# Moving the sums of accumulators by two steps, and reordering the first steps, in a state-space scan joined to a gated MLP

## The chip, the cores and the metric

The kernel runs on one core of a Trainium2 chip. The metric is the device time of one execution in microseconds (us). A core has engines with instruction queues of their own: TensorE (PE in the profile, its weight loads PEld), VectorE (DVE), ScalarE (ACT), GpSimd (POOL) and SyncE (SP, which here only issues DMAs). They wait for one another by semaphores.

## The reference

Two blocks follow each other. The first is a chunked state-space scan over 4 sequences, 8 heads, 768 positions, head width 32 and state width 16. With `C`, `B`, `x` and a decay `a` per position, each chunk gives

```python
M = (C @ B.T) * L                      # L: causal products of decays
y = M @ x + (C @ state) * decay_to_i
state = decay_full * state + sum((B x) * decay_from_j)
```

Its output, arranged as 3072 tokens of width 256, goes into the second block:

```python
h = x @ w_in          # 256 -> 2048
g = h * np.cos(h)
out = g @ w_out       # 2048 -> 256
```

All is float32.

## The kernel before

The 768 positions are cut into six chunks of 128 (the first of them again into two half chunks). Each chunk has 512 tokens over the four sequences. The second block of chunk c is done in 16 steps f = 0 to 15; step n = 16c + f works on 256 of the 512 tokens and on 256 of the 2048 hidden columns. Each step has, in this order of dependence:

- `first(n)` (L705): TensorE multiplies by a part of `w_in` into a PSUM bank `hp`. From step 4 on the `hp` of a step takes one of two banks in turn, so `first(n+2)` needs the bank of step n back.
- `wind_k` (L712, ScalarE) rounds h/2π to an integer `k`, `wind_w` (L718, VectorE) takes the fractional turn `w`, `gate` (L727, ScalarE) takes the cosine as a shifted sine, and `gated` (L732, VectorE) writes `gT` = h cos h from `hp`, after which the bank is free.
- `second(n)`, issued two steps later (`LAG` = 2): TensorE multiplies `gT` by a part of `w_out` into accumulators. In chunk 0 it is a plain product (L776). In chunks 1 to 5 it is a seven-product scheme (`seven`, L814), which needs differences `gd` of `gT`, made by POOL (L757 to L760).

At the last step of each half (f = 7 and f = 15, `second` of which is issued at the end of steps f = 9 and f = 1 of the next chunk), ScalarE copies the seven accumulators to SBUF (L823, L824, tile `ps`) and a closure is put on a list `unsummed`: four VectorE adds (L831, tile `sum`) and two output DMAs (L834). The list is emptied by every step after its `gated`.

While the steps of chunk c - 1 run, the scan of chunk c is woven in. The four sequences go in two pairs, at f = 7 and f = 11. At the end of the step before (f = 6, f = 10): two `reach` scans (L552) and two 32x32 block transposes (L575) on VectorE. In the step: two scaled copies `cT` on ScalarE (L585), `rT` on VectorE (L587), and after the step's `second` 32 small matmuls `g` on TensorE (L602, `intra2`). The masks `m` (L623, VectorE) of a pair's two sequences follow at the end of the next step and in the step after that, ahead of its `gated`. At the end of f = 14 `finish2` multiplies them: `y` (L637, L644), sums for the state (L665).

The two weights are fetched by SP in eight pieces each (in 0 to 7, out 0 to 7) and rounded in the first steps: `grade` takes an absolute value (ScalarE, L254), a clip (POOL, L255) and, as `rest`, a scaled remainder (ScalarE, L252); `join` takes a shift (VectorE, L267), a merge (VectorE, L269) and an addition (POOL, L277) that writes the piece of `w_in` or `w_out`. `first_steps` writes out by hand the order of steps 0 to 3, and the loop from step 4 (`AHEAD` = 4) continues. In step n the loop grades the piece of step n + 1 (odd steps have in (n+3)/2, even ones out n/2) and joins that of step n. `clip_all` (POOL, L920) clips the decays into `la`, which SP stores to DRAM (L923) for later loads. SP issues its DMAs strictly in the order in which the program emits them, and each engine its instructions likewise: no planner moves anything.

The state after the half chunk 1 is completed by `add_s` (POOL, L534 twice and L536), in before at step 6 (`AHEAD + 2`). It is read by `finish0` of half chunk 2 at the end of step 14.

Of the kernel before, what the change touches and what calls it, by code (L numbers as in the profile page):

```python
# [25 lines left out]
def kernel(  # L26
# [21 lines left out]
    NF = DF // P  # L48
# [169 lines left out]
    def kept(which, i):  # L218
        return (w_in[:, :, i * WC:(i + 1) * WC] if which == "in" else
                w_out[:, i * WF:(i + 1) * WF])  # L220
# [12 lines left out]
    held = {}  # L233

    def shares(which, ap, n):

        return [ap] if n == 1 else [ap.rearrange("p (k e f) -> p e k f", k=KT, e=n)[:, e]
                                    for e in range(n)]

    def grade(which, i, later=False, n=1):  # L240


        t = words.pop((which, i), None)
        if t is None:
            return
        mag = conv.tile([P, 2 * WC], FP32, tag="mag", bufs=3, name="mag")
        last = conv.tile([P, 2 * WC], U32, tag="last", bufs=3, name="last")
        low, high, mags, lasts = (shares(which, ap, n) for ap in (t[:, :, 0], t[:, :, 1], mag, last))
        held[which, i] = list(zip(high, shares(which, mag.bitcast(U32), n), lasts))

        def rest(e=0):
            ACT.activation(lasts[e], low[e], AF.Copy, scale=2.0 ** -29)  # L252
        for e in range(n):
            ACT.activation(mags[e], high[e].bitcast(FP32), AF.Abs)  # L254
            G.tensor_scalar(out=mags[e], in0=mags[e], scalar1=MOST, scalar2=LEAST,  # L255
                            op0=ALU.min, op1=ALU.max)
            if not later:
                rest(e)
        if later:
            return rest  # L260

    def join(which, i):


        parts = held.pop((which, i), ())
        for e, (high, bits, last) in enumerate(parts):
            V.tensor_scalar(out=bits, in0=bits, scalar1=3, scalar2=0x3FFFFFFF,  # L267
                            op0=ALU.logical_shift_left, op1=ALU.bitwise_and)
            V.scalar_tensor_tensor(out=bits, in0=high, scalar=0xC0000000, in1=bits,  # L269
                                   op0=ALU.bitwise_and, op1=ALU.bitwise_or)  # L270
            dst = kept(which, i)
            if len(parts) > 1:
                dst = dst[:, :, e * P:(e + 1) * P]
            else:
                bits, last = (ap.rearrange("p (k f) -> p k f", k=dst.shape[1])
                              for ap in (bits, last))
            G.tensor_tensor(out=dst.bitcast(U32), in0=bits, in1=last, op=ALU.add)  # L277
# [10 lines left out]
    for s in range(2):  # L288
# [3 lines left out]
        out=a_in, in_=a.rearrange("(u b) h (c p) -> (b h c) u p", u=NU, p=P))  # L292
# [417 lines left out]
    def wind_k(n):  # L710
        k = ffn.tile([P, TB], I32, tag="k", name="k")
        ACT.activation(k, hp[n], AF.Copy, bias=0.25, scale=INV_2PI)  # L712
        turns[n] = k
# [11 lines left out]
    def gate(n):  # L725
        cos = turns[n]
        ACT.activation(cos, cos, AF.Sin, bias=quarter, scale=TWO_PI)  # L727

    def gated(n):
        cos = turns.pop(n)  # L730
        gT[n] = ffn.tile([P, TB], FP32, tag="gT", bufs=LAG + 1, name="gT")
        V.tensor_tensor(out=gT[n], in0=hp.pop(n), in1=cos, op=ALU.mult)  # L732
        gT[n] = gT[n].rearrange("p (q m) -> p q m", q=4)
        if NF <= n < NC * NF - 1:
            differ(n)
# [104 lines left out]
    unsummed = []  # L840
# [78 lines left out]
    def clip_all():  # L919
        G.tensor_scalar(out=la, in0=a_in, **clip)  # L920
# [6 lines left out]
    piece = {n: ("in", (n + 3) // 2) if n % 2 else ("out", n // 2) for n in range(NF)}  # L927
# [16 lines left out]
    def units_at(n, i):  # L944
        return [k for k, at in unit_at.items() if at[i] == n]
# [47 lines left out]
    AHEAD = 4  # L993

    def first_steps():

        grade("in", 1)
        weigh0(1)
        for q in range(2):
            weights(1, q)  # L1000
        states_of = []
        first(0, lambda: states_of.extend(finish0(1)))
        take_s1, add_s1 = states_of
        join("in", 1)
        rests = [grade("out", 0, later=True)]
        wind_k(0)
        take_s1()
        rests.pop()()
        wind_w(0)
        first(1)  # L1010
        join("out", 0)
        wind_k(1)
        gate(0)
        wind_w(1)
        gate(1)
        gated(0)
        gated(1)
        first(2, tag=None)
        rests = [grade("in", 2, later=True)]
        wind_k(2)  # L1020
        rests.pop()()
        clip_cut()
        wind_w(2)
        rests = [grade("out", 1, later=True)]
        join("in", 2)
        first(3, tag=None)
        gate(2)
        wind_k(3)
        rests.pop()()
        join("out", 1)  # L1030
        gated(2)
        second(0)
        wind_w(3)
        clip_all()
        rests = [grade("in", 3, later=True)]
        gate(3)
        rests.pop()()
        gated(3)
        second(1)
        join("in", 3)  # L1040
        return add_s1

    add_s = first_steps()
    for k in (2, 3):
        G.memset(alongs[k][:, :, 0:1], 0.0)
    rest_of_loads()
    for n in range(AHEAD, NC * NF + LAG):
        c, f = divmod(n, NF)
        if n < NC * NF:

            if c > 0 and f == (NJ if c == 1 else 0):
                if c == 1:
                    load(2, only=(x,))
                load(c + 2)
            if n in (NF - 4, NF + 1):
                for b in range(2):
                    load_a(2, (2 * (n > NF) + b,))
                    load_along(2, (2 * (n > NF) + b,))
            first(n)
            wind(n)  # L1060
            for at in pairs(n):
                turn2(*at)
            for k in units_at(n, 2):
                turn_unit(k)
            rests = [grade(*piece[m], later=True)
                     for m in ((n,) if n == AHEAD else (n + 1,)) if m in piece]
            gate(n)
            for rest in rests:
                if rest:
                    rest()  # L1070
            joins = n > AHEAD and n in piece and piece[n] in held
            if joins:
                join(*piece[n])
            elif n == AHEAD:
                grade(*piece[n + 1])

            behind = [lambda at=at: halved(*at) for at in halves_at(n)]
            behind += [lambda k=k, p=p: decays0(k, p) for k, at in unit_at.items()
                       for p in range(2) if at[0][p] == n]
            behind = [lambda at=(c, 2 * u + 1): masked(*at) for c, u in pairs(n - 2)] + behind  # L1080
            behind = [lambda k=k: weights(k, 1) for k in units_at(n - 1, 3)] + behind
            if not joins and behind:
                behind.pop(0)()
            gated(n)
            if n == AHEAD:
                join(*piece[n])
            if add_s and (n == AHEAD + 2 or units_at(n - 1, 4)):
                add_s()
                add_s = None
            for do in (*behind, *unsummed):  # L1090
                do()
            unsummed.clear()
            for k, ((_, last_), *_) in unit_at.items():
                if last_ == n:
                    weigh0(k)
                    if k == 3:
                        units_of_decay()
        for i, js in differ_at.get(n, ()):
            differ_w(i, js)
        if n >= LAG:  # L1100
            second(n - LAG)
        for c, u in pairs(n - 1):
            intra2(c, u)
            masked(c, 2 * u)
        for k in units_at(n, 3):
            for t in range(2):
                inner(k, t)
            weights(k, 0)
        for k in units_at(n, 4):
            take_s, add_s = finish0(k)  # L1110
            take_s()
        for k in units_at(n, 1):
            reach_unit(k)
        for c, us in ends(n):
            finish2(c, us)
            if 1 in us:
                raw.pop(c)
        for c, u in pairs(n + 1):
            for b in (2 * u, 2 * u + 1):
                reaches(c, b)  # L1120
                load_along(c + 1, (b,))
            turn_blocks(c, u)
        for at, (c, u) in block_loads.items():
            if at == n:
                loading = load_blocks(c, u)
            if at <= n < at + 8:
                next(loading)
# [30 lines left out]
```

## Time and profile before

| What | us |
|---|---|
| median of 3 runs | 375.1 (374.86 to 375.34) |
| the profiled execution | 374.5 |
| its span, first to last instruction | 372.7 |
| TensorE busy in the span | 363.2 |
| VectorE busy | 274.3 |
| POOL busy | 215.6 |
| ScalarE busy | 172.6 |

The time of the profiled execution is of one run; its span leaves out what lies before the first and after the last instruction. Lines of the timeline give the start, the duration, the engine, the line of the kernel, the operation with the tile written and the tiles read, the number of instructions merged, and in brackets the idle time of the engine before it with what ended it. Ends of matmuls are modelled in the profile, so that periods between steps are read from starts.

### The profile page before, as it was taken

What the parts mean: (1) busy time and instruction counts of PE and PEld (TensorE: products, weight loads), DVE (VectorE), ACT (ScalarE), POOL (GpSimd) and SP (SyncE); (2) the same over time, 40 slices, a digit from 0 to 9 for tenths busy, and PEclk for the clock granted to TensorE, in tenths of its full rate; (3) what the DMA queues carried; (4) which work ended last, traced back from release to release, by engine and by line L of the source; (5) the groups of instructions that cost most, each with busy time, mean ns of one, the idle gap of its engine ahead of it and who ended that gap; (6) DMA issues with size and microseconds to landing.
All of it is one profiled execution on the core that took longest, in us unless ns stands there. A gap on an engine that the chain in (4) does not pass through costs nothing.

```text
span 372.7 us, 8684 instructions
## 1 busy us (share of the span) xinstructions
PE 363.2 (97%) x3390; PEld 326.6 (88%) x3390; DVE 274.3 (74%) x451; ACT 172.6 (46%) x299; POOL 215.6 (58%) x339
## 2 busy tenths in 40 slices
PE   8999999999999899999999999999999999999996
PEld 5787878889999799999899999899999989999995
DVE  7788998578699848977857987766987872544543
ACT  3678566553443434444335345433534443444442
POOL 6556855579776547765445684453685344544451
PEclk9999999999999999999999999999999999999999
DMA  9947796666077552530344340110010100010011
GB/s 145 296 163 185 163 272 88 117 162 167 5 144 132 139 76 66 151 91 0 70 55 93 91 135 16 49 24 2 11 38 2 25 5 2 2 28 1 2 30 29
DMA packets 96489, 30.49 MB, mean 82 GB/s; under 512 B 70240, under 2 KB 92352, under 8 KB 96448
## 3 DMA queue, kind: packets, MB, share of 16 engines
q1 hardware_dynamic: 94160, 29.48, 35.0%
q10 hardware_dynamic: 2288, 0.46, 0.6%
q8 instruction: 27, 0.44, 0.5%
q14 instruction: 14, 0.11, 0.1%
HBM read 26.58 MB, written 3.34 MB: 80 GB/s over the span
## 4 chain that ended last, share of the span: by engine, by line
PE 74%; DVE 10%; DMA 4%; ACT 4%; SPq 3%; issue 2%; POOL 1%; DVEq 0%; ACTq 0%; POOLq 0%
PE hp L705 36%; PE o L814 26%; PE o L776 4%; SPq L109 3%; PE y L644 2%; DVE w L718 2%; DVE sum L831 2%; DMA arow<-a_cut 2%; ACT w L727 1%; DMA bc<-in_C_dram 1%; DVE turned L575 1%; DVE gT L732 1%; PE y L637 1%; ACT k L712 1%; DVE reach L552 1%
## 5 line engine op out<-in xcount | busy, mean ns | idle before, releaser
L705 PE MATMUL hp<-yT,w_in 128*128 128x256 f32 x768 | 183.4, 382 | 2.7 <-DVE gT L732 2.6
L705 PEld LDWEIGHTS hp<-yT,w_in 128*128 128x128 f32 x768 | 139.4, 191 | 22.4 <-issue 3.3
L757 POOL TENSOR_TENSOR gd<-gT 128x256 f32<-128x256 f32 x79 | 60.0, 760 | 98.8 <-DVE gT L732 94.8
L727 ACT ACTIVATE w<-w,quarter 128x512 f32<-128x512 f32 x96 | 69.2, 721 | 77.6 <-DVE w L718 77.5
L718 DVE SCALAR_TENSOR_TENSOR w<-hp,k 128x512 f32<-128x512 f32 x96 | 65.7, 685 | 47.0 <-ACT k L712 47.0
L712 ACT ACTIVATE k<-hp 128x512 int32<-128x512 f32 x96 | 57.0, 594 | 75.7 <-PE hp L705 75.4
L732 DVE TENSOR_TENSOR gT<-hp,w 128x512 f32<-128x512 f32 x96 | 65.3, 680 | 35.4 <-ACT w L727 24.0
L814 PE MATMUL o<-words,gd 128*128 128x128 f32 x474 | 66.0, 276 | 0.0
L814 PEld LDWEIGHTS o<-words,gd 128*128 128x128 f32 x474 | 59.3, 192 | 0.0
L814 PEld LDWEIGHTS o<-w_out,gT 128*128 128x128 f32 x316 | 47.5, 191 | 4.1 <-ACT ps L823 0.2
L760 POOL TENSOR_TENSOR gd<-gT,gd 128x128 f32<-128x128 f32 x79 | 44.6, 565 | 6.2
L814 PE MATMUL o<-w_out,gT 128*128 128x128 f32 x316 | 48.1, 275 | 0.0
L759 POOL TENSOR_TENSOR gd<-gT,gd 128x128 f32<-128x128 f32 x79 | 44.0, 557 | 6.2
L561 DVE TENSOR_TENSOR_SCAN lam<-arow,unit 128x512 f32<-128x512 f32 x32 | 42.8, 1338 | 0.0
L776 PE MATMUL o<-w_out,gT 128*128 128x256 f32 x128 | 30.3, 381 | 0.7 <-POOL w_out L277 0.7
L814 PE MATMUL o<-words,gT 128*128 128x128 f32 x158 | 30.6, 275 | 0.0
L814 PE MATMUL o<-w_out,gd 128*128 128x128 f32 x158 | 30.6, 275 | 0.0
L776 PEld LDWEIGHTS o<-w_out,gT 128*128 128x128 f32 x128 | 24.1, 190 | 4.6 <-POOL w_out L277 1.5
L623 DVE TENSOR_TENSOR m<-g,lam 128x256 f32<-128x256 f32 x64 | 24.6, 414 | 0.4
L814 PEld LDWEIGHTS o<-w_out,gd 128*128 128x128 f32 x158 | 24.0, 192 | 0.0
L814 PEld LDWEIGHTS o<-words,gT 128*128 128x128 f32 x158 | 24.0, 192 | 0.0
L831 DVE TENSOR_TENSOR sum<-ps,sum 128x256 f32<-128x256 f32 (+1 forms) x27 | 16.6, 640 | 0.6
(111 smaller groups left out, 280.3 us busy)
## 6 DMA issues: line engine op xcount, KB each, us to landing
arow<-a_cut SPq DMA_DIRECT2D x16, 512.0 KB
words<-in_moe_w_in_dram SPq DMA_DIRECT2D x8, 512.0 KB
words<-in_moe_w_out_dram SPq DMA_DIRECT2D x8, 512.0 KB
out_dram<-sum SPq DMA_DIRECT2D x18, 128.0 KB
xr<-in_x_dram SPq DMA_DIRECT2D x16, 128.0 KB
blocks<-in_B_dram SPq DMA_DIRECT2D x32, 32.0 KB
blocks<-in_C_dram SPq DMA_DIRECT2D x32, 32.0 KB
along<-a_all SPq DMA_DIRECT2D x16, 64.0 KB
```

The costliest lines, as they stand in the source:

```text
L561: V.tensor_tensor_scan(out=lam[c, b][:, hs].rearrange("p h i -> p (h i)"), data0=rows_.rearrange("p h i -> p (h i)"), data1=unit[:, b % 2 ...
L623: V.tensor_tensor(out=m_[js, :, :, is_], in0=g_[js, :, :, is_], in1=l_[js, :, :, is_], op=ALU.mult)
L705: PE.matmul(to_[:, e], lhsT=w_in[:, k, fs], rhs=y[:, k], start=(k == 0), stop=(k == KT - 1), skip_group_check=True)
L712: ACT.activation(k, hp[n], AF.Copy, bias=0.25, scale=INV_2PI)
L718: V.scalar_tensor_tensor(out=w, in0=hp[n], scalar=INV_2PI, in1=k, op0=ALU.mult, op1=ALU.subtract)
L727: ACT.activation(cos, cos, AF.Sin, bias=quarter, scale=TWO_PI)
L732: V.tensor_tensor(out=gT[n], in0=hp.pop(n), in1=cos, op=ALU.mult)
L757: G.tensor_tensor(out=d[:, 0:2], in0=g[:, 1:2].to_broadcast([P, 2, P]), in1=g[:, 3::-3], op=ALU.subtract)
L759: G.tensor_tensor(out=d[:, 2], in0=g[:, 0], in1=d[:, 0], op=ALU.subtract)
L760: G.tensor_tensor(out=d[:, 3], in0=g[:, 2], in1=d[:, 2], op=ALU.subtract)
L776: PE.matmul(o[c, u][:, t], lhsT=g[:, 2 * e + t], rhs=w_out[:, 2 * j + e], start=(j == e == t == 0), stop=(j == NJ - 1 and e == 1), skip_gr ...
L814: PE.matmul(at[q], lhsT=a_[q], rhs=w[q], start=(j == 0 and q in starts), stop=(j == NJ - 1), skip_group_check=True)
```

## The change

It moves instructions and changes none. It has three parts.

In the loop, the list `unsummed` is not emptied in steps f = 10 and f = 11 of a chunk. The sums of a chunk's first half, which were done after the `gated` of f = 10, are so done after that of f = 12.

In `first_steps` and in the loop's step 4, the order of `gated`, `join`, `grade` and `clip_all` changes: in 3 is graded and `gT` 2 written before out 1 is joined; out 2 is graded in step 3 and no longer in step 4; in 3 is joined before `gT` 3; `clip_all` comes last; in step 4 only in 4 is graded, its remainder following in step 5, and out 2 is joined before `gT` 4.

The state after half chunk 1 is completed in step 11 (`NF - 5`), no longer in step 6.

```diff
         rests.pop()()
+        rests = [grade("in", 3, later=True)]
+        gated(2)
         join("out", 1)
-        gated(2)
         second(0)
         wind_w(3)
-        clip_all()
-        rests = [grade("in", 3, later=True)]
         gate(3)
         rests.pop()()
+        rests = [grade("out", 2, later=True)]
+        join("in", 3)
         gated(3)
         second(1)
-        join("in", 3)
-        return add_s1
+        clip_all()
+        return add_s1, rests
...
-            rests = [grade(*piece[m], later=True)
-                     for m in ((n,) if n == AHEAD else (n + 1,)) if m in piece]
+            if n + 1 in piece:
+                rests_of.append(grade(*piece[n + 1], later=True))
             gate(n)
-            for rest in rests:
+            while len(rests_of) > (n == AHEAD):
+                rest = rests_of.pop(0)
                 if rest:
                     rest()
-            joins = n > AHEAD and n in piece and piece[n] in held
+            joins = n in piece and piece[n] in held
             if joins:
                 join(*piece[n])
-            elif n == AHEAD:
-                grade(*piece[n + 1])
...
             gated(n)
-            if n == AHEAD:
-                join(*piece[n])
-            if add_s and (n == AHEAD + 2 or units_at(n - 1, 4)):
+            if add_s and (n == NF - 5 or units_at(n - 1, 4)):
                 add_s()
                 add_s = None
-            for do in (*behind, *unsummed):
+            for do in behind:
                 do()
-            unsummed.clear()
+            if f not in (10, 11):
+                for do in unsummed:
+                    do()
+                unsummed.clear()
```

More of the change, by code (lines that the diff above doesn't have):

```diff
@@ L1029, in first_steps @@
         rests.pop()()
+        rests = [grade("in", 3, later=True)]
+        gated(2)
         join("out", 1)
-        gated(2)
         second(0)
         wind_w(3)
-        clip_all()
-        rests = [grade("in", 3, later=True)]
         gate(3)
         rests.pop()()
+        rests = [grade("out", 2, later=True)]
+        join("in", 3)
         gated(3)
         second(1)
-        join("in", 3)
-        return add_s1
-    add_s = first_steps()
+        clip_all()
+        return add_s1, rests
+    add_s, rests_of = first_steps()
     for k in (2, 3):
```

## The prediction

> **What bounds the kernel now.** I read the page's first lines, then the waits of TensorE, then the timeline around every place where the period between two steps' first matmuls is long.
>
> ```profile
> span 372.7 us, 8684 instructions
> PE 363.2 (97%) x3390; PEld 326.6 (88%) x3390; DVE 274.3 (74%) x451; ACT 172.6 (46%) x299; POOL 215.6 (58%) x339
> ...
> PE hp L705 <- DVE gT L732: 2.6, 5, 0.8
> ```
>
> TensorE is the bound; other engines matter only where it waits. The last line (waits: total, times, longest) says that its largest wait is for a bank of `hp`, which VectorE frees with `gT`: five times, 2.6 us. In the timeline one falls at 52.5 us, the others in step 12 of chunks 1 to 4. Chunk 2:
>
> ```profile
> 163.47 1.89 PE L705 MATMUL hp<-yT,w_in 128*128 128x256 f32 x8
> 167.69 2.00 PE L705 MATMUL hp<-yT,w_in 128*128 128x256 f32 x8
> ...
> 175.26 0.69 DVE L732 TENSOR_TENSOR gT<-hp,w 128x512 f32<-128x512 f32 x1 [0.86 <-ACT w L727]
> 175.86 0.42 DVE L831 TENSOR_TENSOR sum<-ps 128x256 f32<-128x256 f32 x1
> 176.31 1.89 DVE L831 TENSOR_TENSOR sum<-ps,sum 128x256 f32<-128x256 f32 x3
> 177.66 1.89 PE L705 MATMUL hp<-yT,w_in 128*128 128x256 f32 x8
> 178.13 0.73 DVE L552 TENSOR_TENSOR_SCAN reach<-along,ones 128x128 f32<-128x128 f32 x2
> 178.78 1.08 DVE L575 STREAM_TRANSPOSE turned<-blocks 128x256 f32<-128x256 f32 x2
> 179.70 0.68 DVE L718 SCALAR_TENSOR_TENSOR w<-hp,k 128x512 f32<-128x512 f32 x1
> 179.90 0.91 ACT L585 ACTIVATE cT<-turned,slot 128x256 f32<-128x256 f32 x2 [2.93 <-DVE turned L575]
> 181.52 0.69 DVE L732 TENSOR_TENSOR gT<-hp,w 128x512 f32<-128x512 f32 x1 [0.81 <-ACT w L727]
> 182.36 1.97 PE L705 MATMUL hp<-yT,w_in 128*128 128x256 f32 x8 [0.40 <-DVE gT L732]
> ```
>
> Step 8 does the same matmuls for the first pair, without sums, in 167.69-163.47 = 4.22 us. Step 12 takes 182.36-177.66 = 4.70: `gT` of step 11 ends at 182.21, behind sums, scans, transposes, `w` and `rT`. The same difference of starts in chunks 1 to 4: 5.58-4.22 = 1.36, 0.48, 4.67-4.22 = 0.45, 4.68-4.21 = 0.47. Sum 2.76 us.
>
> The other losses lie in chunk 0, where a plain step takes 3.45 us:
>
> ```profile
> 36.18 2.00 PE L776 MATMUL o<-w_out,gT 128*128 128x256 f32 x8 [0.29 <-POOL w_out L277]
> ...
> 46.67 0.69 ACT L254 ACTIVATE mag<-words 128x512 f32<-128x512 f32 x1 [1.75 <-DMA words<-in_moe_w_in_dram]
> 47.26 0.71 ACT L727 ACTIVATE w<-w,quarter 128x512 f32<-128x512 f32 x1
> ...
> 48.00 0.69 DVE L732 TENSOR_TENSOR gT<-hp,w 128x512 f32<-128x512 f32 x1 [0.70 <-ACT w L727]
> 48.61 1.77 DVE L385 TENSOR_TENSOR_SCAN lam<-arow,unit 128x512 f32<-128x512 f32 x1
> 48.86 1.94 PE L705 MATMUL hp<-yT,w_in 128*128 128x256 f32 x8
> ...
> 53.20 1.97 PE L705 MATMUL hp<-yT,w_in 128*128 128x256 f32 x8 [0.67 <-DVE gT L732]
> ```
>
> Steps 4 and 6 lose 0.78 and 0.72 (starts 26.32, 30.55 and 34.01, 38.18): `second` waits for a piece of `w_out` that POOL joins last. Steps 7 to 9 lose 0.33 together (38.18 to 48.86), step 10 0.89. The 46.67 line rules all of this: ScalarE's absolute value of piece in 6 waits for its DMA, and the sine of step 8 stands behind it.
>
> **What the Trainium skill says.** "SBUF — State Buffer", section "Who interferes with whom": VectorE and GpSimd lock one shared pair of ports for a whole instruction. The trace agrees: the join's shift (L267, alone 0.42) took 1.50 from 25.03, while POOL's L277 ran 24.97 to 26.25. "TensorE: Matmul & The Clock Gate", section "Architectural detail: the array is 16× 32×32, not 1× 128×128": ScalarE and VectorE queues are strict FIFO. The 47.26 line agrees: its `w` was ready at 45.79.
>
> **The change part by part, sums.** Nothing is added or removed; four adds (0.42+1.89, 2.34 us from 175.86 to 178.20) move behind `gT` of step 12, nine times in before, at step 10 in five of them. Step 2's four stay. Chunk 5's have no transposes beside them and no stall (its steps 10 to 12 take 3.29): worth nothing. In chunks 1 to 4, by the rows above: `gT` of step 10 ends 175.95, scans to 176.6, transposes to 177.6, `w` (its `k` is there at 176.97) to 178.3, `rT` to 178.7. ScalarE: two `cT` to 178.55, sine to 179.2; `gT` 179.25 to 179.95, against 182.21 now. TensorE's pair of matmuls would end near 181.9, so the bank is free 1.9 us early: the 0.48 goes whole. In chunk 1 a 1.2 us scan (L561) stands ahead of `gT`; from the end of `gT` 10 at 116.87 the walk gives 121.5 against a demand at 122.3: the 1.36 goes whole.
>
> Where the 2.34 us go: chunk 2, `gT` 12 ends 182.4, sums 184.65, first masks (1.40) 186.0, `w` 13 186.6, second masks (1.7) 188.2, `gT` 13 188.95. TensorE, now 0.47 earlier, begins `y` (L637) at 188.6; that needs the first half of the second masks, 187.4; L644 at 189.7 needs all of them, 188.2. Slack 1.2 and 1.5. Chunk 1: halves at 128.9 against 129.05, all at 129.75 against 130.1. Slack only 0.1 to 0.3; I price it at 0 to 0.4 and take 0. Without that cover a late microsecond costs one. `gT` 13 is not wanted until `first` of step 15, at 192. The two output DMAs move with the sums in SP's queue, past along, arow and two block loads (those go out earlier, no longer behind a wait for the sums). Behind the wait stand the remaining block loads, read some 10 steps later: nothing.
>
> **Joins, clips, `gT` of steps 2 to 4.** ScalarE does the absolute value of out 2 before `k` 4 and the remainder of in 4 a step later, so that `k` 5 comes near 32.9, not at 34.00. POOL clips in 3 between two joins: that meets VectorE's L269 at the port. The same meeting at 36.10 (POOL 0.79, L269 0.98) put 1.39 us between two POOL joins; so out 1 is joined near 28.9, not 28.67: step 4 loses 0.24 more. Out 2: absolute value to 30.2, clip to 30.85, then in 3's join to 32.15 and `la` (0.40), L269 to 33.3, in 4's clip to 33.8, join 33.9 to 35.2; now it ends at 36.12. TensorE wants it at 36.0, so step 6 has no wait: -0.72. With the small losses of steps 7 to 9 TensorE could be 0.5 to 0.8 ahead at the end of step 9. There it stops: `first` 10 needs `gT` 8, which hangs on the DMA of in 6. From its issue at 42.43 back, SP's chain is out 4's issue (31.94 to 36.06), `la`'s store at 36.06, loads of `along` waiting for that store, then in 6. No step of it waits for an engine if `la` is there by 36.06; I have it at 32.6 to 33.0 (now 29.15). So `gT` 8 ends at 48.69 and step 10 begins at 48.86 as before. Step 11 waits for `gT` 9 along scan L385 (48.61), `w` 9 and sine 9, all behind `gT` 8: 53.20 again. Worth: 0, bounds 0 and -1.5.
>
> **State 1.** Three POOL operations (1.69+0.87 from 41.41) go from step 6 to step 11. Behind them: the join of out 6 (62.08 to 63.35), then near 64; read by `second` 12 after 66.6. The sum is read by `finish0` at 68.47. VectorE meets them near 61 to 63, up to 0.7 us; `gT` 12 (61.85) has 2.4 us until step 14. Cost 0. At step 6 scan L385 (1.93 at 40.61, 1.2 to 1.4 elsewhere) gets shorter, again ahead of in 6: 0.
>
> **Sum.** -2.76 on the profiled execution of 374.5 us (span 372.7, 1.8 around it): span 369.9, execution 371.7. The median shown is 375.1, 0.6 above the profiled one: 375.1-2.8 = 372.3.
>
> **Rivals.** (1) The lead of chunk 0 is kept: 0.7 to 1.5 more, about 371.2. For it: steps 4 to 9 do lose 1.83. Against: the 1.75 us DMA wait. (2) The stall moves to step 14: if sums or masks take a microsecond longer than walked (both share time with POOL's `gd`), chunk 1 gives back about 1.0 and the others about 0.2 each: about 373.9. For it: chunk 1's slack. Against: 1.2 us elsewhere. (3) Scans or transposes wait for something other than the sums, their loads say, and step 12 stays: 375.1. Against: in step 6 the same operations follow `gT` at once. (4) Slower: `la` now stands behind two ScalarE passes, two clips and a join, and SP stops at its store. From 36.06 every microsecond delays in 6, `gT` 8 and step 10 alike; the gain is eaten at 38.8, slower by 0.75 at 39.6. An absolute value that waited 6.6 us more would do it, about 375.9. Against: out 2 and in 4 were issued at 14.6 and 15.1 and are not waited for now.
>
> **How the numbers follow.** Forecast 0.60 (its own 371.8 to 372.9), rival 1 0.15, rival 2 0.13, rival 3 0.06, rival 4 0.06. What a measurement can tell from no change is 0.2%, 0.75 us. Faster: forecast, rivals 1 and 2, less a little for the worst of rival 2: 0.86; within 0.2%: 0.07; slower: 0.07. Range 371.0 to 374.1: from rival 1 to the far end of rival 2; rivals 3 and 4 are left out.
>
> **What would show it.** Right: step 12 of chunks 1 to 4 takes 4.2 us, `hp` waits for `gT` once (52.5 us) or twice, step 6 takes 3.45, steps 10 and 11 begin at 48.9 and 53.2, step 14 stays at 6.75. Wrong: a wait of L637 or L644 for the masks, step 10 well before 48.8, or `la`'s store after 36.1.

## The result and the profile after

The changed kernel takes 371.03 us (median of 4 runs, 370.93 to 371.4). Runs of the kernel before beside it have a median of 375.02. The ratio is 0.9894, with a 95% interval of 0.9877 to 0.9911. So 4.0 us are gained where 2.8 were forecast. The time lies in the forecast's range of 371.0 to 374.1, but near its lower end: it is the time of rival 1, whose mechanism had been argued against, and the forecast's own 371.8 to 372.9 was missed.

The profiled execution of after took 371.4 us. Its page begins:

```profile
span 369.6 us, 8679 instructions
PE 362.2 (98%) x3390; PEld 326.7 (88%) x3390; DVE 275.9 (75%) x451; ACT 172.7 (47%) x299; POOL 214.7 (58%) x339
```

The engines do the work of before. VectorE is even busier by 1.6 us, which costs nothing. What changed is TensorE's waits. In the list of its waits, the `hp` line that led before (2.6 us, five times) is gone. The wait for `w_out` is still 0.7 in sum, but in one piece instead of two:

```profile
PE o L776 <- POOL w_out L277: 0.7, 1, 0.7
```

**Step 12.** The timeline of chunk 2 in after, the same stretch as was shown of before:

```profile
173.45 0.69 DVE L732 TENSOR_TENSOR gT<-hp,w 128x512 f32<-128x512 f32 x1 [0.86 <-ACT w L727]
174.06 1.24 DVE L552 TENSOR_TENSOR_SCAN reach<-along,ones 128x128 f32<-128x128 f32 x2
...
175.86 1.89 PE L705 MATMUL hp<-yT,w_in 128*128 128x256 f32 x8
177.97 0.69 DVE L732 TENSOR_TENSOR gT<-hp,w 128x512 f32<-128x512 f32 x1 [0.81 <-ACT w L727]
180.08 1.99 PE L705 MATMUL hp<-yT,w_in 128*128 128x256 f32 x8
181.18 1.89 DVE L831 TENSOR_TENSOR sum<-ps,sum 128x256 f32<-128x256 f32 x3
184.92 1.74 DVE L623 TENSOR_TENSOR m<-g,lam 128x256 f32<-128x256 f32 x4
186.86 1.10 PE L637 MATMUL y<-rT,state 32*64 32x128 f32 x32
187.89 1.95 PE L644 MATMUL y<-m,xr 128*32 128x128 f32 x64
```

Step 12 runs from 175.86 to 180.08, which is 4.22 us, the time of step 8. The `gT` that frees the bank (177.97 to 178.66) is done 1.4 us before the bank is wanted. The forecast had 1.9: its walk gave the two `reach` scans 0.65 us, and they take 1.24. They do follow `gT` of step 10 at once, so that rival 3 did not come. The sums now stand at 181.18, behind the next `gT`. The second masks end at 186.66. L637 begins at 186.86 with no bracket, so it waited for nothing that the profile shows.

**Chunk 0.** From the timeline of after:

```profile
29.80 1.99 PE L776 MATMUL o<-w_out,gT 128*128 128x256 f32 x8 [0.66 <-POOL w_out L277]
...
46.05 0.67 ACT L254 ACTIVATE mag<-words 128x512 f32<-128x512 f32 x1 [1.54 <-DMA words<-in_moe_w_in_dram]
...
48.90 1.89 PE L705 MATMUL hp<-yT,w_in 128*128 128x256 f32 x8
...
52.57 1.97 PE L705 MATMUL hp<-yT,w_in 128*128 128x256 f32 x8
```

Steps 10 and 11 seem to begin where they did before, at 48.9 and near 53. That is deceptive. Executions of this program reach step 3 at different times, for reasons that the change doesn't touch: 21.14 in before, 21.98 in after, 24.19 in an experiment below that has the code of before up to step 6. (These starts are of single matmuls in the trace; the timeline merges steps 2 and 3 into one line.) One part of it shows in the waits ahead of step 3: TensorE's wait at L405 for POOL's `c` is 0.2 us in before and 0.9 in after. That step 10 begins at 48.9, as the forecast's sign said, is so chance. Times in chunk 0 are told from the start of step 3. On that clock step 10 begins at 26.92 in after and 27.72 in before, and step 11 at 30.59 against 32.06. Chunk 0 gained 1.47 us.

The two spans agree with this. Step 12 of chunks 1 to 4 took 5.59, 4.69, 4.68 and 4.68 us and takes 4.22 four times, which is 2.76 less. With 1.47 of chunk 0 it makes 4.23. Against it stand the later step 3 (0.84) and 0.28 us in pieces of at most 0.1 in other steps. The sum is 3.1, and the spans differ by 372.7 - 369.6 = 3.1.

### The profile page after: what moved, and what is told of

It is laid out like the page before. It is cut to its first block, busy times and chain, and to the rows that moved or that the text cites. A ratio compares the mean times of both kernels' runs of the same rounds, so it can differ in the third digit from the quotient of the medians.

```text
span 369.6 us, 8679 instructions
## 1 busy us (share of the span) xinstructions
PE 362.2 (98%) x3390; PEld 326.7 (88%) x3390; DVE 275.9 (75%) x451; ACT 172.7 (47%) x299; POOL 214.7 (58%) x339
## 4 chain that ended last, share of the span: by engine, by line
PE 93%; DVE 2%; ACT 2%; DMA 2%; issue 1%; POOL 1%; ACTq 0%
PE hp L705 44%; PE o L814 33%; PE o L776 7%; PE y L644 2%; PE g L602 2%; DMA bc<-in_C_dram 2%; PE y L637 1%; PE g L466 1%; PE y L508 1%; DVE mag L267 1%; PE y L491 1%; PE o L859 1%; PE y L500 0%; DVE mag L269 0%; PE s_ps L665 0%
## 5 line engine op out<-in xcount | busy, mean ns | idle before, releaser
L718 DVE SCALAR_TENSOR_TENSOR w<-hp,k 128x512 f32<-128x512 f32 x96 | 65.7, 684 | 45.0 <-ACT k L712 44.8
L776 PE MATMUL o<-w_out,gT 128*128 128x256 f32 x128 | 30.2, 380 | 0.7 <-POOL w_out L277 0.7
L776 PEld LDWEIGHTS o<-w_out,gT 128*128 128x128 f32 x128 | 24.2, 190 | 4.3 <-POOL w_out L277 1.1
```

What stands on the lines that cost most here:

```text
L718: V.scalar_tensor_tensor(out=w, in0=hp[n], scalar=INV_2PI, in1=k, op0=ALU.mult, op1=ALU.subtract)
L776: PE.matmul(o[c, u][:, t], lhsT=g[:, 2 * e + t], rhs=w_out[:, 2 * j + e], start=(j == e == t == 0), stop=(j == NJ - 1 and e == 1), skip_gr ...
```

## The experiments

**One part alone, and the others without it.** The sums alone, in the kernel before:

```diff
-            for do in (*behind, *unsummed):
+            for do in behind:
                 do()
-            unsummed.clear()
+            if f not in (10, 11):
+                for do in unsummed:
+                    do()
+                unsummed.clear()
```

> The kernel before with the sums alone moved from step 10 to step 12. Theory 1 (the sums are worth the waits of step 12, 2.76 us, and the order of the first steps brings the rest): 2.7 to 2.8 us below before, about 372.3, steps 12 of chunks 1 to 4 at 4.22 us, chunk 0 as before with step 10 starting where the piece in 6 lets it. Theory 2 (the first steps bring nothing and the sums are worth all 4.0 us): 371.0.

The changed kernel with this edit taken back, so that the orders and state 1 remain:

> The changed kernel with the sums back in step 10. Theory 1: 1.2 us below before, about 373.8, and step 6 at 3.45 us; step 12 of chunk 1 still 5.6. Theory 2, which the prediction made (all that the first steps gain is given back at step 10, where the DMA of in 6 decides): 375.0, with the abs of in 6 ending its DMA wait at the same time in both kernels.

The same with state 1 back in step 6, so that only the orders of the first steps remain:

```diff
-            if add_s and (n == NF - 5 or units_at(n - 1, 4)):
+            if add_s and (n == AHEAD + 2 or units_at(n - 1, 4)):
```

> The first steps in the new order, the state after half chunk 1 still completed in step 6, sums in step 10. If the state's place brings nothing: as the kernel with both, 373.8 if theory 1 holds. If the state's three POOL operations, which stretch a scan and hold back the clip of out 4 in step 6, cost part of it: 0.3 to 0.7 us more than that one.

And the reverse of that last edit alone, in the kernel before:

> The kernel before with the state after half chunk 1 completed in step 11 alone. Expected by the prediction: 0, within 0.3 us of 375.0, step 10 starting at the same time as in the kernel before. If the state's place is what let step 10 start earlier: 0.6 to 1.2 us less.

| Kernel | median, us | ratio to before (95%) | step 12 of chunks 1 to 4, us | step 3 to step 11, us |
|---|---|---|---|---|
| before | 374.88 | | 5.59, 4.69, 4.68, 4.68 | 32.06 |
| sums alone | 372.48 | 0.9928 (0.9909 to 0.9947) | 4.22 four times | 31.87 |
| orders and state 1 | 373.39 | 0.9954 (0.9937 to 0.9970) | 5.59, 4.69, 4.69, 4.67 | 30.36 |
| orders alone | 373.78 | 0.9968 (0.9956 to 0.9980) | 5.58, 4.69, 4.67, 4.69 | 30.51 |
| state 1 alone | 374.55 | 0.9998 (0.9983 to 1.0014) | 5.57, 4.69, 4.67, 4.68 | 31.59 |

(The ratios pair the runs, so that they differ a little from the quotients of the medians.) The sums bring 2.4 and the rest 1.5; together 3.9, and the whole change brings 4.0. The parts add up. What state 1 brings is not settled. Alone its interval holds 1, though its median is 0.33 us below that of before. In the new order the runs with it (373.08 to 373.72 us) lie almost wholly below those without it (373.64 to 374.26), 0.4 between the medians. In the traces step 3 to step 11 is 0.47 and 0.15 us shorter with it, but the sums alone, which do not touch that stretch, differ from before by 0.19 too. So it may be worth up to some 0.4 us; no stall that it removes was found. The forecast for the sums stands, its zero for the first steps does not.

**The cover of the sums.** The sums were costed at nothing because slack before L637 hides them. To find where that ends, the four adds of the first half were done twice in after; the second set writes the same values again:

```diff
-            for dst, a_, b_ in ((sum_[:, 0:2], ps[:, 1:3], ps[:, 0:1]),
+            for dst, a_, b_ in (2 if u == 0 else 1) * (
+                                (sum_[:, 0:2], ps[:, 1:3], ps[:, 0:1]),
```

> The changed kernel with the four adds of a chunk's first half done twice in step 12, 2.34 us more of VectorE there. If the cover is the slack of the y matmuls against the masks, 1.06 us in chunks 2 to 4 (first half of the second masks at about 185.8, L637 at 186.86) and 0.2 in chunk 1, step 14 grows by 1.3 us in chunks 2 to 4 and by 2.1 in chunk 1: 5.9 us in all, about 376.9. If y waits for all of the masks of both sequences only at L644: 1.1 and 2.0, 376.3. If there is cover left that the walk does not see: under 374.

It took 375.02 us, ratio 1.0002 (0.9993 to 1.0011): the whole gain is gone. From its waits of TensorE, and its timeline in chunk 2:

```profile
PE y L637 <- DVE m L623: 2.6, 4, 1.3
```

```profile
182.44 1.90 DVE L832 TENSOR_TENSOR sum<-ps,sum 128x256 f32<-128x256 f32 x3
184.25 0.41 DVE L832 TENSOR_TENSOR sum<-ps 128x256 f32<-128x256 f32 x1
184.70 1.09 DVE L832 TENSOR_TENSOR sum<-ps,sum 128x256 f32<-128x256 f32 x3
187.63 1.75 DVE L623 TENSOR_TENSOR m<-g,lam 128x256 f32<-128x256 f32 x4
188.62 1.10 PE L637 MATMUL y<-rT,state 32*64 32x128 f32 x32 [0.44 <-DVE m L623]
```

Rival 2's wait appears where it was placed: L637 waits for masks. Step 14 grew by 1.37 in chunk 1 and by 0.51, 0.50 and 0.50 in the next three. In the last chunk it grew by 1.00, with a wait of 0.8 us of `first` for `gT`, which the expectation left out. The sum is smaller than the expected 5.9 us because the second set is shorter than the first: 184.25 to 185.79 is 1.5 us, where a set took 2.34. POOL's `gd` operations end at 184.18, so the first set shares its time with them and the second does not. The Trainium skill, "SBUF — State Buffer", section "Who interferes with whom", has VectorE and GpSimd locking one shared pair of ports; the same three adds at 1.90 and at 1.09 us agree.

This gives the slack. In after, the second masks begin at 184.92 and the half that L637 needs is done 0.85 us later, at 185.77, which is 1.1 us before L637 begins at 186.86. In the kernel with doubled sums that half ends at 187.63 + 0.85 = 188.48, and L637 starts at 188.62. So 1.5 us more, minus 1.1, should cost some 0.4 us in chunks 2 to 4, and it cost 0.5. In chunk 1, where after shows some 0.2 us of slack, it should cost 1.3, and it cost 1.37. (The ends of halves are of single instructions in the trace; a line of the timeline merges the four masks.)

**What the first steps hang on.** In 6, whose landing the forecast took to rule step 10, was issued earlier, ahead of the store of `la`, in before and in after:

```diff
         fetch("out", 4)
+        fetch("in", 6)
         store_a(a_all, la)
...
         load_unit_along(2)
-        fetch("in", 6)
```

> The kernel before with the fetch of in 6 put ahead of the store of la, so that it lands near 40 us and not at 46.6. If step 10's start hangs on that landing, as the prediction says: no DMA wait before the abs of in 6, step 10 earlier by 0.3 to 0.9 us against the start of step 3, step 11 still held by out 5, together 0.5 to 1.2 us below before. If the landing does not decide: 375, unchanged.

> The changed kernel with in 6 fetched ahead of the store of la. In its trace step 10 loses only 0.22 us and nothing else waits in steps 5 to 9, so at most 0.2 us below the changed kernel: 370.8 to 371.1. If the changed kernel still lost time to that DMA in its unprofiled runs: 0.5 us or more below it.

And later, in after, behind the two loads of `x` that follow it:

```diff
         load_unit_along(2)
-        fetch("in", 6)
         for s in range(2):
             load_x(2, s)
+        fetch("in", 6)
```

> The changed kernel with the fetch of in 6 behind the two loads of x, 1.3 us later in SP's queue. By the prediction's mechanism (gT 8 hangs on that landing): in 6 lands 1.2 to 1.4 us later against step 3, step 10 starts 0.5 to 0.8 us later and step 11 1.1 to 1.4 us later, 372.1 to 372.4, which is the time predicted for the change itself. If the landing has room to spare: 371.0.

Early in before: 374.62, ratio 0.9994 (0.9986 to 1.0003); no change that can be told. Early in after: 371.17, 0.9900 (0.9884 to 0.9917), as without it. Late in after: 372.75, 0.9934 (0.9916 to 0.9953), 1.7 us lost, more than expected. The timeline of the late one, in which step 3 begins at 21.50:

```profile
47.61 0.66 ACT L254 ACTIVATE mag<-words 128x512 f32<-128x512 f32 x1 [3.58 <-DMA words<-in_moe_w_in_dram]
...
49.75 1.97 PE L705 MATMUL hp<-yT,w_in 128*128 128x256 f32 x8 [1.18 <-DVE gT L732]
...
54.12 1.97 PE L705 MATMUL hp<-yT,w_in 128*128 128x256 f32 x8 [0.67 <-DVE gT L732]
```

ScalarE waits 3.58 us for the piece, and TensorE then waits at step 10 and at step 11. Its issue comes 1.5 us later against step 3 than in after and its landing 2.0 us later, where 1.2 to 1.4 were expected; step 11 follows 2.0 us later. So the chain of the prediction is real: in 6, absolute value, sine, `gT` 8, step 10. But in 6 did not land when the prediction said. ScalarE's wait for it ended 25.5 us after the start of step 3 in before and 24.1 in after, with nothing in the change that touches its DMA. And in before, an early in 6 shortens step 3 to step 11 by 0.35 us (31.71 against 32.06) and not by the expected 0.5 or more: VectorE's own queue, which runs there without a gap from 45.48 to 53.08, holds `gT` 9 and with it step 11 nearly as long.

**Why SP's queue ran earlier.** Two neighbouring issues of SP carry it. Their lines in SP's timeline of before, and then of after:

```profile
28.50 3.34 SPq L124 DMA_DIRECT2D bc<-in_B_dram  x2
31.94 4.08 SPq L230 DMA_DIRECT2D words<-in_moe_w_out_dram  x1
```

```profile
29.64 1.99 SPq L124 DMA_DIRECT2D bc<-in_B_dram  x2
31.74 3.52 SPq L230 DMA_DIRECT2D words<-in_moe_w_out_dram  x1
```

The two loads of `B` take 1.35 us less to issue and out 4 takes 0.56 less, though no semaphore is waited for. Out 4's issue ends 14.9 us after the start of step 3 in before and 13.3 in after; in 6 is issued 1.35 us earlier. What the DMA engines did meanwhile shows in the view of DMA of the stretch from 30 to 38 us (one digit is 0.2 us, 9 is 90% busy or more), of before:

```profile
DMA  9649788999999999999998510000000002989977
...
q8 instruction: 1, 0.02, 0.8%
```

and of after:

```profile
DMA  9865349857879999999999999999999407997999
```

In before, the DMA engines stand almost idle for 2 us, from 34.6 to 36.6, while SP is inside the issue of out 4 or has just left it. In after this hole is 0.2 us. The other difference is the `q8` line, a fetch of instructions, one packet of 16 KB. It is taken to be TensorE's: in before the queue has 27 such packets, and between two of them TensorE executes 249 instructions (matmuls, weight loads, semaphores) on average over the whole span. By the trace's packets this fetch came 11.50 us after the start of step 3 in before, among the densest loads, and 2.48 us after it in after, when the DMA engines were idle. This made a new theory (F below): TensorE's instruction stream, not an engine's work, sets how fast SP's issues go here. Its rival (G): the stream has nothing to do with it, and the new order of POOL, VectorE and ScalarE by itself lets the loads through.

Two kernels tell them apart. The first is before with 16 tiny matmuls put ahead of the transposes in `turn_c`, written to `tp` and overwritten there; no other engine's order changes, only TensorE's instruction stream shifts:

```diff
+        for _ in range(16):
+            PE.matmul(tp[0:32, 0, 0:4], lhsT=ones[:, 0:32], rhs=ones[:, 0:4], start=True,
+                      stop=True, skip_group_check=True)
```

> The kernel before with 16 tiny matmuls (32 columns, overwritten later) where TensorE idles near 6.5 us, so that its instruction stream is 64 instructions further on and its 16 KB instruction fetch, which in all three kernels of the old order falls 11.0 to 11.5 us after the start of step 3 into the busiest stretch of the DMAs, comes earlier. Theory F (the fetches that share the DMA engines hold back the loads; in the new order that fetch comes 2.4 to 2.8 us after step 3): the issue of out 4 ends 0.5 to 1.2 us earlier after step 3 than the 14.5 to 14.9 of the old order, in 6 lands earlier by as much, and the time is 0.3 to 0.9 us below before. Theory G (the fetch is a bystander): out 4's issue still ends at 14.5 to 14.9 and the time is that of before.

The second is after with one pair of lines swapped back, in `first_steps`:

```diff
-        gated(2)
         join("out", 1)
+        gated(2)
```

> The changed kernel with one pair swapped back: out 1 joined ahead of gT 2 on VectorE. The second of step 2 then waits for two semaphores again (gT 2 and the piece), so that TensorE's sequencer stops there, as in the kernel before. Theory F: the 16 KB instruction fetch goes back to 11 to 11.5 us after the start of step 3, the issue of out 4 ends at 14.5 to 14.9 and not at 13.3, in 6 lands 1.0 to 1.4 us later, steps 10 and 11 lose that: 0.7 to 1.3 us above the changed kernel, 371.7 to 372.3. Theory G (the fetch is a bystander, the engines' order alone decides): within 0.3 us of the changed kernel.

The swapped-back kernel takes 372.45, ratio 0.9925 (0.9910 to 0.9940), so one pair of lines is worth 1.2 us by the ratios and 1.4 between the medians. Its issue of out 4 in SP's timeline, and its view of DMA from 30 to 38 us:

```profile
32.28 4.33 SPq L230 DMA_DIRECT2D words<-in_moe_w_out_dram  x1
```

```profile
DMA  4964676999999999999999983100000000009223
...
q8 instruction: 1, 0.02, 0.8%
```

The fetch is back, 11.71 us after the start of step 3. The hole is back with 2.2 us, and the issue of out 4 ends at 15.4.

The shifted kernel as a whole is slower, 382.04 (1.0192, 1.0177 to 1.0208), by a cost of its own ahead of step 3 that is told in the last section. But past step 3 it answers the question. In its view of DMA from 36.8 to 44.8 us (7.8 to 15.8 us after its step 3; the views above reach from 8.9 to 16.9 in before and from 8.0 to 16.0 in after):

```profile
DMA  9999747946899999999999999999420063999998
```

The hole has shrunk to 0.4 us and the stretch has no fetch of TensorE; that came 4.7 us ahead of step 3. The issue of out 4 ends at 13.3 with the order of before on all other engines. That step 3 comes later here leaves no older loads behind or ahead: in this kernel as in before, after and the swapped one the DMA engines carry nothing from 4.5 to 5.5 us after the start of step 3, and the loads start from rest. The rival fits neither kernel: here the other engines keep the order of before and the delay is gone.

All kernels fall into the same two groups (by one trace of each). Where the fetch came 11.0 to 11.7 us after the start of step 3 (before, sums alone, state 1 alone, in 6 early in before, and the swapped one), the issue of out 4 ended at 14.5 to 15.4. Where it came at 2.9 or sooner (after and its other variants, and the shifted one), it ended at 13.3 to 13.8. Both conditions are needed for the gain:

| Step 3 to step 11, us | in 6 lands late | in 6 lands early |
|---|---|---|
| old order of the first steps | 32.06 (before) | 31.73 (shifted), 31.71 (in 6 issued early) |
| new order | 32.46 (swapped back), 32.62 (in 6 issued late) | 30.59 (after), 30.36 (in 6 issued early) |

The new order with a late in 6 gains nothing, as the prediction said; the old order with an early one gains 0.3; both together gain 1.5.

What stays open. Why the swap moves the fetch was only argued: with out 1's join ahead of `gT` 2, TensorE has a semaphore instruction of its own at L776, 6.7 to 7.0 us after the start of step 3, in every kernel of the old order (the shifted one too) and in the swapped one, and none there in the others. That TensorE, when it isn't stopped there, asks for its next instructions sooner is a guess that no run shows.

How the fetch holds SP back is open too. In before the packet begins at 11.50 after step 3, but the issue of the loads of `B` ends at 10.70, already 1.05 us later than in after. So the packet's own microsecond can't be the cause of that part. And in all five kernels with a late fetch the packet begins 0.69 us after SP begins to issue out 4, whether that is at 10.33 (sums alone) or at 11.02 (swapped back): its time follows SP's queue, or both follow a third thing. If the fetch was asked for when the semaphore was passed, it lay in wait from 6.8 to 11.5, over both issues; after shows 1.1 us from its last semaphore to the packet on idle engines. The trace has no record of the request.

Of the hole the trace shows more. In before, from 13.8 to 15.4 us after step 3, its 125 packets go in single file: each begins 3 to 10 ns before the one ahead ends, and never are more than two in flight. That is what one DMA engine that has fallen behind would give, with the others done and SP still held in its issue. Which engine that is, and what put it behind, is not recorded. Shown is that a shift of TensorE's stream alone, and one swap that moves its fetch, decide over the delay.

**The clip between two joins.** The step that the new order was said to make worse is step 4. In after, in 3 was graded later, behind out 1's join, with `gT` 2 still ahead:

```diff
-        rests = [grade("in", 3, later=True)]
         gated(2)
         join("out", 1)
+        rests = [grade("in", 3, later=True)]
```

> The changed kernel with the clip of in 3 on POOL behind the join of out 1, gT 2 still ahead of it. If the clip costs step 4 its 0.24 us by the shared port: step 4 back at 4.23, 0.0 to 0.25 us below the changed kernel (less if step 10 takes it back), 370.8 to 371.0. If the clip's later place makes in 3 late: 371.2 or more.

371.26, ratio 0.9899 (0.9877 to 0.9921): the same as after. Step 4 does go back from 4.47 to 4.24 us, so the clip between the joins is what had lengthened it. But TensorE then meets in 6 that much earlier, and step 10 takes 3.98 instead of 3.67; step 3 to step 11 is 30.70.

## Why the prediction was right or wrong

- **Sums.** Right in mechanism and size. Step 12 was to take 4.2 and takes 4.22 in all four chunks; the term of 2.76 is 2.76 in the traces and the sums alone gave 2.4 between the medians, 2.0 to 3.4 by the interval of the ratio.
- **The slack that hides them.** Right. For chunks 2 to 4 it was put at 1.2 us and measures 1.1, for chunk 1 at 0.1 to 0.3 and measures 0.2. Step 14 stays at 6.75. Rival 2 did not come, and the doubled sums show it waiting just beyond. The walk of these 2.34 us past masks, `w` and `gT` was good to 0.3 us; the statement that without cover a late microsecond costs one held too.
- **Steps 4 and 6.** Right: step 4 was to lose 0.24 more and lost 0.23 (4.24 to 4.47), step 6 was to gain 0.72 and gained it (4.17 to 3.45), and steps 7 to 9 gained the 0.33. `la` ends at 33.36, which on before's clock is 32.5, where 32.6 to 33.0 was said. Rival 4 did not come: SP stores `la` at 35.3, 1.9 us after it is there.
- **"There it stops."** This step failed, and with it the worth of 0. It said that the lead ends at in 6, that no step of SP's chain waits for an engine, and that step 10 so begins as before. The first two hold: in 6 issued late costs 1.7 us. But that SP's chain waits for no engine does not make its times fixed. The issues of out 4 and of the loads of `B` ahead of it held 1.4 to 1.6 us that depend on where TensorE's instruction stream stands, as the shifted and the swapped kernel show, and the new order moved that. The term was bounded at 0 to -1.5 and measured -1.47, the far end. The time lies in the range, by 0.03 us, only because the range left room for rival 1; this part was luck.
- **Rival 1** gave the time, 371.2 against 371.03, by keeping the lead of 0.7 to 1.5. What was held against it, the DMA wait of 1.75 us, fell: that wait is 1.54 in after, but it ends 1.5 us earlier against step 3.
- **State 1.** Not settled. Its cost of 0 was right in that nothing got slower, but it may have gained up to some 0.4 us. One reading was wrong: scan L385 at step 6 was to get shorter without POOL's three operations beside it, and it took 1.93 us in before and takes 1.91 in after. (The 1.2 to 1.4 that it was compared with are not its own: the other three of these L385 scans in before take 1.35 to 2.08.)

## What to carry to other kernels

Where a lead is said to stop at a transfer, ask what in the transfer's own chain is a duration and not a wait, and whether the change can move it: an issue that lasts 4 us in SP's queue is a symptom, and the view of DMA over that stretch, with its instruction queue, is where to look for what it depends on. Small operations behind the bound engine can be moved for nothing as far as the slack of their new place reaches, which here was 0.2 us in one chunk and 1.1 in the next three; measure it by doubling them. Compare stretches from an event that both kernels share, not from the start of the span, when executions reach that event at different times.

## What the runs showed of the hardware

Instructions reach TensorE over the DMA engines that also carry the data: the 27 packets of 16 KB on `q8` are counted among the traffic of the core's 16 DMA engines. In this program a late fetch, about 1 us long among the densest loads, went with a hole of some 2 us in nearly all DMA traffic and with 1.4 us of delay for in 6 in SP's queue. The Trainium skill, "DMA: Bandwidth & Descriptors", section "Queues, rings and completion order", says that each DMA engine serves its rings in turn, a packet at a time; that a fetch stands among loads fits this, but no run here shows the turn itself.

TensorE itself can stand still without a wait that the profile shows. The shifted kernel, in TensorE's timeline ahead of step 3:

```profile
21.62 0.43 PE L511 MATMUL y<-m,xr 64*32 64x64 f32 x4 [3.04 <-issue]
21.98 8.92 PE L708 MATMUL hp<-yT,w_in 128*128 128x256 f32 x28
```

Between two matmuls of one group it stood 3.04 us for no semaphore, and the 28 matmuls that follow took 8.92 us where before has 6.31 for as many. That is 5.7 of the 7.9 us by which step 3 comes later; the tiny matmuls themselves took 1.0 us where they stand. A fetch of 16 KB lies within the 3.04 us (19.24 to 20.24) and another among the 28 matmuls (from 24.29); that they are the cause was not tried.
